# Joining two half inverses in three slots of a hand-ordered attention and MLP kernel

## The chip, the cores and the metric

One NeuronCore of a Trainium2 chip. The metric is device time in microseconds (us) of one execution, lower is better. Three runs of the kernel before stand at 674.85, 675.14 and 677.65; the median is 675.14.

## The reference

A delta rule with memory runs over 768 tokens for 4 x 8 heads of 48 dimensions, and its output is the input of a gated MLP (384 to 1536 to 384):

```python
for t in range(S):
    y[:, :, t] = np.einsum('bhd,bhde->bhe', q[:, :, t], state)
    v_old = np.einsum('bhde,bhd->bhe', state, kt)
    state = state + bt[:, :, :, None] * np.einsum('bhd,bhe->bhde', kt, vt - v_old)
...
gate = 1.0 / (1.0 + np.exp(-(x @ w_gate)))
return (gate * (x @ w_val) @ w_out)
```

with `kt` a row of k divided by its norm. Everything is float32.

## The kernel before

**Work.** The tokens are cut into N = 12 groups of 64 tokens a batch (256 rows of the MLP each). In a group the delta rule becomes matrix work: a Gram matrix of the keys (`gram`, L253), norms (`norms`, L206), the inverse of a triangular matrix of 64 x 64 per head, held as two 32 x 32 blocks on the diagonal (`mt`) and one block beside it (`L`), the corrected values U (`rest` L376 to L394, `updates` L396), the output Y (`rows`, L421), the new state (`advance`, L450) and a transposition of Y into the two-part operand `xx` of the MLP (`flip`, L469). The MLP of a group runs in NF = 12 tiles of 128 hidden units: `gate_val` (18 matmuls, L492), `gated` (sigmoid on ScalarE L497, product on VectorE L498), `split_hi` (L503), `split_lo` (L508) and `outp` (6 matmuls, L518).

**Slots.** The order of every engine's instructions is written out by hand: `slot(s)` (L673) is called for s = 0, 1, 2 ... and each engine works through its own instructions strictly in that order. An even slot issues `gate_val` of tile s/2, then the list `plan[s]`, then `split_lo` of the tile before and `gated` of its own tile, then the list `late[s]`. An odd slot issues `outp` of the tile that is two back, `plan[s]`, `split_hi`, `late[s]`. Slots 0 to 23 run the MLP of group 0, 24 to 47 that of group 1, and so on. In this document "tile 6" is the tile of slot 12, and "tile 12" the first tile of group 1, in slot 24.

**What is in `plan` up to slot 24.** The MLP's weights come as raw words and are converted in the first 21 slots: `converting` (L196) gives 97 steps, some 4.6 a slot, of which two in three run on VectorE (`join` L184, `weight_lo` L194) and one on ScalarE (`weight_hi` L189); `scaled` (L164) gives two more ScalarE passes a piece up to slot 15, a small POOL copy (L176) and the load of a later piece on SP's queue. `gate_val(f)` needs the pieces that were converted one or two slots earlier.

**Group 1's inverse.** For groups 0 and 1 `solve_halves` (L327) inverts two halves of 16 rows and joins them. Norms and halves of group 1 are one generator of NORMS + HALVES = 18 + 40 = 58 steps, which `spread` (L540) deals out evenly over slots 0 to 11. Its last six steps are two copies of the halves into `X` (L353, after a memset of X on POOL, L351), and then the joining:

```python
nc.vector.transpose(mt..., X...)          # L355, and with it
blocks(pz, A, mt)                         # L362: 128 small matmuls, then a step ends
nc.vector.transpose(D..., mt...)          # L365
nc.scalar.copy(Z, pz)                     # L366, a step ends
blocks(pm, D, Z)                          # L362: 128 small matmuls, a step ends
nc.vector.tensor_tensor(out=mt, in0=mt, in1=pm, op=ALU.subtract)   # L370
```

All six fall into slot 10 (the first of them) and slot 11 (the other five), in `plan`, so before `split_lo` and `gated` of slot 10, and before `split_hi` of slot 11. They depend on each other in turn: VectorE, TensorE, ScalarE, TensorE, VectorE.

**What follows for group 1.** `updates(1, 0)`, `(1, 1)` and `(1, 2)` stand in `late` of slots 13, 15 and 17, `rows(1)` and `advance(1)` in slot 19, both `flip(1, c)` in slot 21; `gate_val` of tile 12 in slot 24 needs `xx` of group 1.

**Group 2's inverse** is a single chain of 18 + 66 = 84 VectorE steps (`norms`, `solve` L296) over slots 16 to 32. The share of a slot is weighted by `max(0.1, 1.6 - busy[s])`, and `busy` (a table of extra VectorE work by slot) is filled from `up` and `at_rows`, the slots of U and Y. It ends with the transposition into `mt` (L319), which `updates(2, 0)` in slot 34 needs (L413).

Of the kernel before, what the change touches and what calls it, by code (L numbers as in the profile page):

```python
# [55 lines left out]
def deltanet_gated_mlp(ctx: ExitStack, tc: tile.TileContext, kd, qd, kv, beta, words, out):  # L56
# [107 lines left out]
    def scaled(n):  # L164

        half, lo, hi = words_of(n)
        nc.scalar.activation(lo.bitcast(I32), half, AF.Copy, bias=-4095.5 / 8192, scale=1 / 8192)
        h = hi.bitcast(F32)  # L170
        nc.scalar.activation(h, h, AF.Prelu, scale=2.0 ** -112, alpha=-2.0 ** 32)
        later = n + AHEAD
        if later < len(pieces):

            raw[later] = wt.tile([128, PW, 2], U32, name=f"raw_{later}", tag=f"w{later}")
            nc.gpsimd.tensor_copy(out=raw[later][0:1, 0:1, 0], in_=raw[n][0:1, 0:1, 1])  # L176
            load_piece(later)
# [28 lines left out]
    def norms(g):  # L206


        st = state[g]
        st["gp"] = gp = wk.tile([128, 32, 32], F32, name=f"gp_{g}", tag="gp", bufs=1)  # L210
        nc.vector.transpose(gp.rearrange("q t (c r) -> q t c r", r=2), st["G"].unsqueeze(3).to_broadcast([128, 32, CP, 2]))
        yield
        ss = gp.rearrange("q t c -> q (t c)")[:, 0:32 * 32:33]
        t1, y, t, s, m = (wk.tile([128, 32], F32, name=f"{x}_{g}", tag=x, bufs=1) for x in ("n1", "ny", "nt", "ns", "m"))
        nc.vector.tensor_scalar(out=t1.bitcast(I32), in0=ss.bitcast(I32), scalar1=1, scalar2=None, op0=ALU.logical_shift_right)
        yield
        nc.vector.tensor_scalar(out=y.bitcast(I32), in0=t1.bitcast(I32), scalar1=-1.0, scalar2=float(0x5f375a00), op0=ALU.mult, op1=ALU.add)
        yield
        for _ in range(2):
            nc.vector.scalar_tensor_tensor(out=t, in0=y, scalar=-0.5, in1=y, op0=ALU.mult, op1=ALU.mult)  # L220
            yield
            nc.vector.tensor_tensor(out=t, in0=t, in1=ss, op=ALU.mult)
            yield
            nc.vector.scalar_tensor_tensor(out=y, in0=t, scalar=1.5, in1=y, op0=ALU.add, op1=ALU.mult)
            yield
        nc.vector.tensor_tensor(out=s, in0=y, in1=ss, op=ALU.mult)
        yield
        nc.vector.scalar_tensor_tensor(out=t, in0=s, scalar=-1.0, in1=s, op0=ALU.mult, op1=ALU.mult)
        yield
        nc.vector.tensor_tensor(out=t, in0=t, in1=ss, op=ALU.add)  # L230
        yield
        nc.vector.scalar_tensor_tensor(out=t, in0=t, scalar=0.5, in1=y, op0=ALU.mult, op1=ALU.mult)
        yield
        nc.vector.scalar_tensor_tensor(out=m, in0=t, scalar=EPS, in1=s, op0=ALU.add, op1=ALU.add)
        yield
        nc.vector.tensor_tensor(out=t, in0=m, in1=m, op=ALU.mult)
        yield
        st["gam"] = gam = wk.tile([128, 32], F32, name=f"gam_{g}", tag="gam", bufs=2)
        nc.vector.reciprocal(gam, t)
        yield  # L240
        nc.vector.tensor_tensor(out=gam, in0=gam, in1=st["beta"], op=ALU.mult)
        yield
        st["mq"] = mq = wk.tile([128, CP, 2], F32, name=f"mq_{g}", tag="mq", bufs=1)
        nc.vector.transpose(mq.rearrange("p c r -> p (c r)"), m)
        yield
# [81 lines left out]
    def solve_halves(g):  # L327


        st = state[g]  # L330
        gp, gam = st["gp"], st["gam"]
        X = wk.tile([128, 16, 32], F32, name=f"X_{g}", tag="X", bufs=1)
        H = wk.tile([128, 2, 8, 16], F32, name=f"H_{g}", tag="H", bufs=1)
        gs = wk.tile([128, 2, 16, 16], F32, name=f"gs_{g}", tag="gs", bufs=1)
        A, D, Z = (scratch[:, i] for i in range(3))
        for b in range(2):
            nc.vector.tensor_tensor(out=H[:, b], in0=dmask[:, 8 * b:8 * b + 8, 16 * b:16 * b + 16],
                                    in1=gam[:, 16 * b:16 * b + 16].unsqueeze(1).to_broadcast([128, 8, 16]), op=ALU.mult)
            yield
            nc.vector.scalar_tensor_tensor(out=gs[:, b], in0=gp[:, 16 * b:16 * b + 16, 16 * b:16 * b + 16], scalar=-1.0,  # L340
                                           in1=gam[:, 16 * b:16 * b + 16].unsqueeze(1).to_broadcast([128, 16, 16]), op0=ALU.mult, op1=ALU.mult)
            yield
        for j in range(15, 0, -1):
            k, n = j // 2, 8 - j // 2
            tmp = wk.tile([128, 2, n, j], F32, name=f"tmp_{g}_{j}", tag="tmp", bufs=2)
            nc.vector.tensor_tensor(out=tmp, in0=H[:, :, k:8, j:j + 1].to_broadcast([128, 2, n, j]),
                                    in1=gs[:, :, j:j + 1, 0:j].to_broadcast([128, 2, n, j]), op=ALU.mult)
            yield
            nc.vector.tensor_tensor(out=H[:, :, k:8, 0:j], in0=H[:, :, k:8, 0:j], in1=tmp, op=ALU.add)
            yield  # L350
        nc.gpsimd.memset(X, 0.0)  # L351
        for b in range(2):
            nc.vector.tensor_copy(out=X[:, 8 * b:8 * b + 8, 16 * b:16 * b + 16], in_=H[:, b])  # L353
            yield
        nc.vector.transpose(mt.rearrange("q c (k r) -> q k c r", r=2), X.rearrange("q k (c r) -> q k c r", r=2))  # L355
        pool, tag = (ps_aux, "aux") if g else (ps_gv, "gv")
        pz, pm = (pool.tile([128, CP, 32], F32, name=f"{n}_{g}", tag=tag) for n in ("pz", "pm"))

        def blocks(out, lhsT, rhs):
            for c in range(CP):  # L360
                for r in range(0, 128, 32):
                    nc.tensor.matmul(out=out[r:r + 32, c], lhsT=lhsT[r:r + 32, c], rhs=rhs[r:r + 32, c], start=True, stop=True)  # L362
        blocks(pz, A, mt)
        yield
        nc.vector.transpose(D.rearrange("q c t -> q (c t)"), mt.rearrange("q c t -> q (c t)"))  # L365
        nc.scalar.copy(Z, pz)  # L366
        yield
        blocks(pm, D, Z)
        yield
        nc.vector.tensor_tensor(out=mt, in0=mt, in1=pm, op=ALU.subtract)  # L370
        yield
# [159 lines left out]
    plan = collections.defaultdict(list)  # L531
    late = collections.defaultdict(list)

    def steps(gen, n=1):
        def fn():
            for _ in range(n):
                next(gen, None)
        return fn

    def spread(gen, total, lo, hi, room=lambda s: 1.0):  # L540

        done, upto, whole = 0, 0.0, sum(room(s) for s in range(lo, hi))
        for s in range(lo, hi):
            upto += total * room(s) / whole
            n = total if s == hi - 1 else round(upto)
            plan[s].append(steps(gen, n - done))
            done = n

    def chain(*gens):
        for q in gens:  # L550
            yield from q
# [10 lines left out]
    NORMS, SOLVE, HALVES = 18, 66, 40  # L562
# [52 lines left out]
    spread(conv, 3 * len(pieces) - 11, 0, W - 3)  # L615
    for n in range(11, len(pieces)):
        plan[max(0, (n - 12) * 2 // 3)].append(lambda n=n: scaled(n))
    spread(chain(norms(1), solve_halves(1)), NORMS + HALVES, 0, 12)
    for s in (4, 5):
        plan[s].append(steps(scalings[1], 8))  # L620
    for part in (1, 0):
# [21 lines left out]
    for g in range(N):  # L643
        w = W * (g - 1)
        if g == 0:
            late[3].append(lambda: advance(0))
            continue
        up, at_rows = (13, 19) if g == 1 else (10, 16)
        late[w + 6].append(lambda g=g: rest(g))
        for step in range(3):  # L650
            late[w + up + 2 * step].append(lambda g=g, step=step: updates(g, step))
        late[w + at_rows].append(lambda g=g: rows(g))
        late[w + at_rows].append(lambda g=g: advance(g))
        for c in range(2):
            late[w + at_rows + 2].append(lambda g=g, c=c: flip(g, c))
            busy[w + at_rows + 2] += 0.6
        busy[w + 6] += 1.1
        busy[w + up + 2] += 1.1
        busy[w + at_rows] += 1.1
        busy[w + at_rows + 1] += 1.1  # L660
        if g == 1:
            mask_later(1, 1)
        else:
            if g > 2:
                plan[w - 27].append(lambda g=g: load_group(g))
            gram_later(g, w - 18)
            mask_later(g, w + 1 if g == 2 else w - 12)
            solves.append((g, w - 8 if g == 2 else w - 14, w + 9))
            scaling(g, w - 3 if g == 2 else w - 7)
# [72 lines left out]
```

## Time and profile before

| | |
|---|---|
| median of three runs | 675.14 us |
| time of the profiled execution | 674.84 us |
| its span, first to last instruction | 673.1 us |
| around the span (difference) | 1.74 us |
| TensorE (PE) busy | 617.6 us (92%) |
| VectorE (DVE) busy | 481.3 us (72%) |
| ScalarE (ACT) busy | 322.9 us (48%) |
| GpSimd (POOL) busy | 16.0 us (2%) |
| granted TensorE clock, mean | 0.980 |

The chain of work that ended last runs 77% of the span on PE, 11% on DVE, 5% in issue. A share over the span says little here, as the first 160 us and the rest are two different stages: in the first the weights are converted and the first groups' inverses are made, in the second the MLP runs from weights that lie ready. The profile gives for each instruction when it started, how long it took, how long its engine sat idle before it and what ended that idle time.

### The profile page before, as it was taken

To read this page: it belongs to the slowest core of one execution; us is meant where nothing else is said; L and a number is where in the kernel's file an instruction comes from. 1 tells how busy PE (TensorE), PEld (TensorE's weight loads), DVE (VectorE), ACT (ScalarE), POOL (GpSimd) and SP (SyncE) were. 2 spreads that over 40 slices of the span, in tenths; PEclk is the share of its full clock that TensorE was granted. 3 is DMA by queue.
4 is the path that set the end of the run, shared out by engine and by line. 5 is a ranking of instruction groups with operands and counts; after the bars stand their busy time and mean duration, and the time that the engine had idled before them with its cause. 6 is when DMAs were issued, how large, how long until landed. Compare 5 with 4: busy or idle time off the path is not lost.

```text
span 673.1 us, 24164 instructions
## 1 busy us (share of the span) xinstructions
PE 617.6 (92%) x10504; PEld 595.4 (88%) x10504; DVE 481.3 (72%) x1480; ACT 322.9 (48%) x881; POOL 16.0 (2%) x57
## 2 busy tenths in 40 slices
PE   5278829898999999999999999999999999999996
PEld 4267728788999999999999999999999999999996
DVE  4469857998797797797797787786886886862221
ACT  5748957435535524534534444444444354433322
POOL 5001100000000000000000000000000000000000
PEclk9999869898999999999999999999999999999999
DMA  8565540210210210210220220220220110010101
GB/s 257 182 224 166 196 160 2 81 27 24 82 24 26 83 24 26 81 42 10 81 48 3 81 50 2 81 49 4 81 49 27 58 25 3 1 25 3 24 1 24
DMA packets 17770, 41.07 MB, mean 61 GB/s; under 512 B 4224, under 2 KB 7296, under 8 KB 17664
## 3 DMA queue, kind: packets, MB, share of 16 engines
q1 hardware_dynamic: 17664, 39.53, 20.2%
q8 instruction: 82, 1.34, 0.8%
q14 instruction: 24, 0.20, 0.1%
HBM read 34.80 MB, written 4.72 MB: 59 GB/s over the span
## 4 chain that ended last, share of the span: by engine, by line
PE 77%; DVE 11%; issue 5%; ACT 3%; DMA 2%; SPq 1%; POOL 0%; ACTq 0%; DVEq 0%; POOLq 0%
PE gv L492 41%; PE po L518 22%; PE pu L413 3%; DVE w L194 2%; PE yy L439 2%; PE yy L442 2%; PE pp L286 1%; PE pk L382 1%; DVE u L184 1%; DMA raw<-in_words_dram 1%; PE pd L460 1%; PE pk L405 1%; PE pt L478 1%; PE pg L262 1%; DVE tmp L314 1%
## 5 line engine op out<-in xcount | busy, mean ns | idle before, releaser
L492 PE MATMUL gv<-xx,w 128*128 128x256 f32 x2592 | 343.7, 287 | 7.0 <-DVE w L194 5.0
L492 PEld LDWEIGHTS gv<-xx,w 128*128 128x128 f32 x2592 | 335.2, 194 | 10.4 <-DVE w L194 5.8
L518 PE MATMUL po<-w,h 128*128 128x384 f32 x864 | 182.7, 346 | 0.7 <-DVE h L508 0.7
L497 ACT ACTIVATE sg<-gv 128x256 f32<-128x256 f32 x144 | 55.3, 384 | 198.5 <-PE gv L492 198.3
L518 PEld LDWEIGHTS po<-w,h 128*128 128x128 f32 x864 | 145.5, 189 | 5.3 <-DVE h L508 1.8
L498 DVE TENSOR_TENSOR sg<-sg,gv 128x256 f32<-128x256 f32 x144 | 60.2, 418 | 76.3 <-ACT sg L497 75.9
L503 ACT CAST h<-sg 128x256 fp32r<-128x256 f32 x144 | 58.4, 405 | 69.0 <-DVE sg L498 67.5
L317 DVE TENSOR_TENSOR X<-X,tmp 128x126 f32<-128x126 f32 (+22 forms) x310 | 79.1, 255 | 9.8
L314 DVE TENSOR_TENSOR tmp<-X,gp 128x126 f32<-128x126 f32 (+22 forms) x310 | 78.8, 254 | 9.0
L508 DVE TENSOR_TENSOR h<-sg,h 128x256 fp32r<-128x256 f32 x144 | 60.0, 416 | 27.5 <-ACT h L503 27.5
L419 ACT COPY su<-pu 32x384 f32<-32x384 f32 x92 | 43.3, 471 | 13.6 <-PE pu L413 12.3
L250 ACT ACTIVATE kv<-kv,mq 128x48 f32<-128x48 f32 x192 | 48.1, 330 | 0.0
L467 DVE TENSOR_TENSOR su<-su,pd 48x384 f32<-48x384 f32 x40 | 22.1, 552 | 21.1 <-PE pd L460 20.6
L270 ACT COPY G<-pg 32x256 f32<-32x256 f32 (+1 forms) x72 | 26.5, 368 | 18.5 <-PE pg L262 17.2
L291 DVE TENSOR_TENSOR kqp<-pp,pmask 64x512 f32<-64x512 f32 x48 | 32.1, 686 | 1.2 <-PE pp L286 0.2
L393 DVE TENSOR_TENSOR R<-kv,pk 128x384 f32<-128x384 f32 x44 | 22.4, 550 | 1.8 <-PE pk L382 1.8
L189 ACT CAST w<-u 128x384 fp32r<-128x384 f32 x36 | 17.7, 512 | 11.2 <-DVE u L184 11.1
L413 PE MATMUL pu<-R,mt 32*32 32x48 f32 x1408 | 19.7, 202 | 3.0 <-DVE mt L319 1.9
L413 PEld LDWEIGHTS pu<-R,mt 32*32 32x32 f32 x1408 | 16.6, 105 | 6.4 <-issue 2.3
L362 PE MATMUL pz<-mt,scratch 32*32 32x32 f32 x256 | 3.9, 236 | 19.3 <-DVE mt L355 19.3
L362 PEld LDWEIGHTS pz<-mt,scratch 32*32 32x32 f32 x256 | 3.7, 151 | 19.8 <-issue 19.8
L262 PE MATMUL pg<-kqp 48*64 48x64 f32 x768 | 16.2, 235 | 5.2 <-DMA kqp<-in_kd_dram 5.2
(86 smaller groups left out, 476.4 us busy)
## 6 DMA issues: line engine op xcount, KB each, us to landing
raw<-in_words_dram SPq DMA_DIRECT2D x36, 384.0 KB, 4.1
kv<-in_kv_dram SPq DMA_DIRECT2D x24, 384.0 KB, 5.2
kqp<-in_qd_dram SPq DMA_DIRECT2D x24, 256.0 KB, 3.8
kqp<-in_kd_dram SPq DMA_DIRECT2D x24, 192.0 KB, 3.6
out_dram<-ot SPq DMA_DIRECT2D x48, 96.0 KB, 2.2
beta<-in_beta_dram SPq DMA_DIRECT2D x12, 16.0 KB, 4.5
```

The lines of the kernel that those rows point to most:

```text
L250: nc.scalar.activation(V[:, c], V[:, c], AF.Copy, scale=mq[:, c, 0:1])
L291: nc.vector.tensor_tensor(out=kq[t:t + 64, sec], in0=pp[e][t:t + 64], in1=pmask[t:t + 64, e].unsqueeze(1).to_broadcast([64, J, C]), op=ALU ...
L314: nc.vector.tensor_tensor(out=tmp, in0=X[:, k:16, j:j + 1].to_broadcast([128, n, j]), in1=gp[:, j:j + 1, 0:j].to_broadcast([128, n, j]), o ...
L317: nc.vector.tensor_tensor(out=X[:, k:16, 0:j], in0=X[:, k:16, 0:j], in1=tmp, op=ALU.add)
L413: nc.tensor.matmul(out=pu[0 if g else x][r:r + 32, j], lhsT=mt[r:r + 32, e * J + j], rhs=R[e][r:r + 32, j], start=True, stop=True)
L419: nc.scalar.copy(su[r:r + 32, 3 if x else e], pu[0][r:r + 32])
L492: nc.tensor.matmul(out=pg[:, o], lhsT=parts[w, f][:, a, k * 128:(k + 1) * 128], rhs=x[b][:, k], start=(k == 0 and q == 0), stop=(k == KC - ...
L497: nc.scalar.activation(h, st["gv", f][:, 0], AF.Sigmoid)
L498: nc.vector.tensor_tensor(out=h, in0=h, in1=st["gv", f][:, 1], op=ALU.mult)
L503: nc.scalar.copy(hh[:, 0], st["sg", f])
L508: nc.vector.tensor_tensor(out=hh[:, 1], in0=st["sg", f], in1=hh[:, 0].bitcast(F32), op=ALU.subtract)
L518: nc.tensor.matmul(out=po[s], lhsT=hh[:, a, ts], rhs=parts["o", f][:, w], start=(f == 0 and q == 0), stop=(f == NF - 1 and q == 2))
```

## The change

The first 55 of the 58 steps are dealt out over slots 0 to 10 (five a slot), so that slot 10 ends with the transposition L355 and the first 128 matmuls. Step 56 (L365 and L366) goes to the end of slot 11 (`late`), step 57 (the second 128 matmuls) to the end of slot 12 (`late`), step 58 (L370) into `plan` of slot 13. U, Y and the flips of group 1 move by one slot: 14, 16, 18 for the updates, 20 for `rows` and `advance`, 22 for the flips. Through `busy` this also changes how the 84 steps of group 2's inverse are dealt out.

```diff
-    spread(chain(norms(1), solve_halves(1)), NORMS + HALVES, 0, 12)
+    first = chain(norms(1), solve_halves(1))
+    spread(first, NORMS + HALVES - 3, 0, 11)
+    for s in (11, 12):
+        late[s].append(steps(first))
+    plan[13].append(steps(first))
...
-        up, at_rows = (13, 19) if g == 1 else (10, 16)
+        up, at_rows = (14, 20) if g == 1 else (10, 16)
```

## Rows read from the trace of the kernel before

**Rows 1.** The page, busy tenths in 40 slices of 16.8 us.

```profile
PE   5278829898999999999999999999999999999996
...
DVE  4469857998797797797797787786886886862221
```

**Rows 2.** Waits of PE, 50 to 170 us: us in total, times, longest.

```profile
PE pz L362 <- DVE mt L355: 10.1, 1, 10.1
```

**Rows 3.** Waits of PE, 166 us to the end.

```profile
PE pd L460 <- issue: 0.7, 2, 0.4
```

**Rows 4.** Waits of DVE, 84 to 160 us.

```profile
DVE mt L370 <- PE pm L362: 6.2, 1, 6.2
DVE sg L498 <- ACT sg L497: 5.0, 3, 2.7
DVE X L353 <- POOL X L351: 1.3, 1, 1.3
```

**Rows 5.** Timeline, slots 10 to 12: start, length, instruction, idle before and releaser.

```profile
90.91 0.23 DVE L353 COPY X<-H 128x128 f32<-128x128 f32 x1 [1.30 <-POOL X L351]
...
93.50 0.71 DVE L355 STREAM_TRANSPOSE mt<-X 128x512 f32<-128x512 f32 x1
94.25 0.71 DVE L365 STREAM_TRANSPOSE scratch<-mt 128x512 f32<-128x512 f32 x1
...
94.36 1.93 PE L362 MATMUL pz<-mt,scratch 32*32 32x32 f32 x128 [10.14 <-DVE mt L355]
...
99.75 1.38 PE L362 MATMUL pm<-scratch 32*32 32x32 f32 x83 [1.91 <-issue]
...
101.06 3.29 PE L492 MATMUL gv<-xx,w 128*128 128x256 f32 x18
101.17 0.69 DVE L370 TENSOR_TENSOR mt<-mt,pm 128x512 f32<-128x512 f32 x1 [6.21 <-PE pm L362]
```

**Rows 6.** Timeline of DVE and ACT, slots 12 to 22.

```profile
104.99 0.42 DVE L498 TENSOR_TENSOR sg<-sg,gv 128x256 f32<-128x256 f32 x1 [1.26 <-ACT sg L497]
...
106.57 1.96 ACT L419 COPY su<-pu 32x384 f32<-32x384 f32 x4
...
111.68 0.42 DVE L498 TENSOR_TENSOR sg<-sg,gv 128x256 f32<-128x256 f32 x1 [2.75 <-ACT sg L497]
```

**Rows 7.** Timeline of DVE, slots 21 to 34.

```profile
134.78 1.02 DVE L481 TENSOR_TENSOR xx<-pt,xx 128x384 fp32r<-128x384 f32 x2 [0.49 <-ACT xx L480]
...
137.79 0.41 DVE L498 TENSOR_TENSOR sg<-sg,gv 128x256 f32<-128x256 f32 x1
...
158.99 0.71 DVE L319 STREAM_TRANSPOSE mt<-X 128x512 f32<-128x512 f32 x1
```

**Rows 8.** Timeline of PE, slots 24 to 36.

```profile
135.85 2.31 PE L492 MATMUL gv<-xx,w 128*128 128x256 f32 x17 [0.29 <-DVE xx L481]
...
154.56 1.22 PE L518 MATMUL po<-w,h 128*128 128x384 f32 x6
155.62 2.32 PE L492 MATMUL gv<-xx,w 128*128 128x256 f32 x18
159.85 0.88 PE L413 MATMUL pu<-R,mt 32*32 32x48 f32 x64 [1.91 <-DVE mt L319]
160.66 1.96 PE L518 MATMUL po<-w,h 128*128 128x384 f32 x6
162.41 3.23 PE L492 MATMUL gv<-xx,w 128*128 128x256 f32 x18
```

**Rows 9.** Stretches: length, busy us of PE, PEld, DVE, ACT, POOL, PEclk, DMA share, GB/s.

```profile
134.00:138.00 4.00, 2.68 (x20) 2.34 (x19) 3.27 (x13) 3.19 (x12) 0.00 (x0) 1.00 0.00 0
...
162.40:165.60 3.20, 3.20 (x23) 3.07 (x22) 1.71 (x8) 1.15 (x3) 0.00 (x0) 0.67 0.02 5
```

**Rows 10.** The page: engines' busy time and instructions; the instruction queue (packets, MB, share).

```profile
PE 617.6 (92%) x10504; PEld 595.4 (88%) x10504; DVE 481.3 (72%) x1480; ACT 322.9 (48%) x881; POOL 16.0 (2%) x57
...
q8 instruction: 82, 1.34, 0.8%
```

## The prediction

> **What bounds the kernel now.** I read first the busy tenths [rows 1]. PE stands at 9 from the eleventh slice on, that is from about 168 us; in the slices before, DVE is the fuller engine and PE has holes. The waits of PE confirm the border: after 166 us it waited 0.7 us in all [rows 3], before that it waited 10.1 us at one place, the first small matmuls of the joining [rows 2]. So whatever PE gains before about 166 us, it keeps to the end; nothing behind that can give or take much.
>
> Next I asked what holds PE before the border. The 10.1 us are not a price by themselves: PE had run ahead of DVE, which converts the weights, and only stood until DVE came. What counts is the time that DVE stands still, because DVE's list up to the transposition of group 2's inverse (158.99 us) ends last: PE's matmuls on it wait for it until 159.85 us, with 1.91 us idle [rows 7, 8]. The waits of DVE between 84 and 160 us are 12.5 us in three kinds [rows 4], and 0.5 for the flips [rows 7]. The largest, 6.2 us, is the change's subject: at 94.96 us DVE has made both transpositions, then PE does 128 small matmuls, ACT copies, PE does 128 more, and only at 101.17 us can DVE subtract [rows 5]. In the second 128 PE itself stands 1.91 us with nothing that the profile names as releaser. Behind it come 1.26 and 2.75 us, DVE waiting for the sigmoids of tiles 6 and 7 [rows 6], and the flips' 0.49. From the joining on that makes 6.21 + 1.26 + 2.75 + 0.49 = 10.7 us of idle DVE.
>
> The profiled execution took 674.84 us (673.1 of span and 1.74 around it), 0.3 us under the median of the three runs; I make the sum against 674.84. A measurement of this kernel tells about 0.5%, 3.4 us, from no change.
>
> **The change, part by part.** No instruction is added or taken away, and none of the moved steps issues a DMA. The loads of group 3 in slot 21, on SP's queue, wait for `rows(1)` and `advance(1)` as before, and their data is used some ten slots later: 0. POOL's memset keeps its place behind slot 10's small copies, and DVE still waits for it; two small steps move ahead of slot 10, and I allow 0.4 us for them (0 to 0.5).
>
> *First transposition and first 128 matmuls, now in slot 10.* At 90.91 us DVE starts the first copy into X. Between that and L365 at 94.25 us it does the second copy, L355, the pair L508 and L498 and three conversion steps [rows 5]. The same seven now stand in another order: L355 follows the two copies and starts at about 91.4. PE's 128 matmuls run from 92.2 to 94.15, 2.1 us earlier. L365 still starts at 94.25.
>
> *Slots 11 and 12.* In place of waiting, DVE goes on with slot 12's three conversion steps and the split, 1.9 us, to 96.9. It needs tile 6's sigmoid next. PE, in order, has `outp` of tile 3 and then tile 6 behind the 128 matmuls, and has been idle, so I price both as the rows after an idle stretch show them: 1.75 us (160.66 to 162.41) and 3.2 us [rows 5, 8]. That ends at 99.1, the sigmoid 0.4 later. DVE waits 2.6 us here, where before it waited 6.21 and 1.26.
>
> *Second 128 matmuls (end of slot 12) and subtraction (slot 13).* They need D and Z, ready at about 95, so PE runs them right behind tile 6: 99.1 to 101.3. DVE, after the product of 0.34 and three conversion steps, comes to the subtraction at about 101.4. Wait: 0, if the 1.91 us of [rows 5] do not recur. Queued behind a late subtraction would be all of slot 14's conversion, for which `gate_val` waits. Why the stall goes: instructions come by a queue of their own, 82 packets of 16 KB for PE's 21,008 matmuls and weight loads, or 256 instructions a packet [rows 10]; the joining hands PE 512 of them in under 4 us, and now `outp` and tile 6 stand between the halves. The other end is that the stall stays with the second half: 1.9 us. I take 0, as nothing else in the rows would hold PE there. The Trainium skill's page "Runtime: NRT & Kernel Launch", section "Instruction fetch mechanics", says that blocks of 256 instructions are streamed ahead and that crossing one is mostly hidden. By that page the 1.91 us would be of another kind and would stay; the trace has a hole of just that size, so I do not go by it in the sum, and the case has its place among the rivals.
>
> *Tile 7's sigmoid.* Before, DVE waited 2.75 us because ACT had the four copies of `updates(1, 0)`, 1.96 us, ahead of it [rows 6]. They now stand in `late` of slot 14, behind that sigmoid. What is left is 0.8; DVE comes earlier against ACT's two `scaled` passes, so I take 1.2 (0.8 to 2.75).
>
> *Updates, rows and flips one slot later.* The matmuls and copies are the same. PE has slack there, since it waits for conversions. The price falls on the flips: L481 now stands behind slot 22's pair and steps. Before, DVE finished L481 at 135.80 and slot 22 at 138.20, 2.4 us [rows 7]. By the new `busy`, 30 of the 84 steps are done by then and not 33, three steps or 0.7 us less; by the end of slot 30 the counts are equal (70). So `xx` is ready 1.7 us later in DVE's list. The flips' wait of 0.5 us I leave in.
>
> *Sum for DVE.* 10.7 - 2.6 - 0 - 1.2 - 0.5 - 0.4 = 6.0 us earlier.
>
> *Sum for PE.* Tile 12 starts at 135.85 + 1.7 - 6.0 = 131.55. Its wait, 1.3 us now (2.68 us busy of 4.00), grows to about 3, and an idle stretch of 1.91 us at 158 was followed by a granted clock of 0.67 (part of the stretch at 1.2 GHz, part at 2.4), while tile 12's present wait was not [rows 8, 9]. The low level costs 0.7 on `outp` (1.75 against 1.06 start to start) and 0.9 on the tile (3.23 against 2.32), 1.6 us [rows 8]. From tile 12 to the end of slot 34 PE has 22.1 us of work without a hole (135.85 to 157.94). So it reaches `updates(2, 0)` at 131.55 + 22.1 + 1.6 = 155.25. DVE's transposition ends at 159.70 - 6.0 = 153.7: no wait is left there, and the 1.6 us that the low level cost behind it are gone. The gain is 159.85 - 155.25 + 1.6 = 6.2 us, and the time 674.84 - 6.2 = 668.6.
>
> **The rivals.**
> (1) *The clock stays up at tile 12.* For it: the hole there may be shorter than 3 us or fall as the present one did [rows 9]. Then PE reaches slot 34 at 153.65, DVE at 153.7, and the gain is 6.1 + 1.6 = 7.7: 667.1.
> (2) *The stall of 1.9 us stays with the second 128 matmuls.* DVE waits 1.8 at the subtraction, its sum falls to 4.2, the gain to 4.4: 670.4. For it: its cause is not shown. Against: the hole lies in the middle of two like blocks that ran back to back.
> (3) *The wait is exchanged for others.* ACT's wait for tile 7 stays at 2.75 as well, and tiles 8 and 9 each add 0.5 (what the flips cost DVE now) because PE is behind: 1.55 + 1.0 more, the gain 1.9: 672.9, no change that can be told. For it: both pz and tile 6 now lie in one queue on PE that DVE waits for. Against: in slots 16 to 20 DVE had no wait for PE or ACT [rows 4, 6, 7].
> (4) *PE takes over at the low clock and the kernel gets slower.* Each new hole (before pz, tile 10, tile 12) could start a stretch at 1.2 GHz, and with PE's work per two slots raised by 1.6 us it, not DVE, would set the pace from slot 11 on. Eleven tiles to slot 34 make 17.6 us, of which 3.2 are in the sum: 6.2 - 14.4 = -8.2, or 683.0. It decides from about six tiles beyond the two counted. Against: after the hole of 158 us the level was back for the second tile [rows 8, 9].
>
> **How the numbers follow.** My forecast has 0.60, (1) 0.13, (2) 0.13, (3) 0.10, (4) 0.04. Forecast, (1) and (2) are faster by over 0.5% of 675.14, which is below 671.8: 0.86. (3) is the same: 0.10. Slower: 0.04. The range runs from 666.7, (1) with POOL's 0.4 not needed, to 671.6, (2) with 1.2 us of the doubt on tile 7's sigmoid; it leaves out (3), (4) and little else.
>
> **What would show it.** Right: DVE's 6.2 us wait for the second matmuls gone or under 0.5; a wait of 2 to 3 us for tile 6's sigmoid; the second 128 matmuls without a hole; tile 12's wait for L481 near 3 us with the clock below 1 behind it; PE's wait for group 2's `mt` gone and `updates(2, 0)` near 155. Wrong: DVE's idle sum behind 90 us above 8, or `updates(2, 0)` after 158, or a new wait of PE behind 166 us.

## The result and the profile after

The changed kernel takes 668.62 us (median of 4 runs, 668.24 to 669.96) against 675.0 of the kernel before (674.78 to 677.65): a ratio of 0.9905 with a 95% interval of 0.9884 to 0.9927. The forecast was 668.6, faster. The profiled execution took 668.93 us; its span is 667.2 us, 5.9 less than before.

The waits of DVE in the changed kernel, 84 to 155 us, answer to [rows 4]:

```profile
DVE sg L498 <- ACT sg L497: 4.4, 3, 2.7
DVE X L353 <- POOL X L351: 1.6, 1, 1.6
DVE kqp L291 <- PE pp L286: 1.1, 1, 1.1
DVE w L194 <- ACT w L189: 0.5, 1, 0.5
```

(Each line: us in total, times, longest.) The 6.2 us before the subtraction (L370) are gone. Two small waits are new: 1.1 us for the masks of group 2 in slot 25 (L291) and 0.5 us in slot 16 (L194). The timeline of slots 10 to 14 shows the joining in its new places ([rows 5, 6]; start, length, instruction, idle before and releaser):

```profile
91.50 0.36 DVE L353 COPY X<-H 128x128 f32<-128x128 f32 x2 [1.63 <-POOL X L351]
91.90 0.71 DVE L355 STREAM_TRANSPOSE mt<-X 128x512 f32<-128x512 f32 x1
...
94.69 0.71 DVE L365 STREAM_TRANSPOSE scratch<-mt 128x512 f32<-128x512 f32 x1
...
99.94 0.42 DVE L498 TENSOR_TENSOR sg<-sg,gv 128x256 f32<-128x256 f32 x1 [2.71 <-ACT sg L497]
...
102.41 0.68 DVE L370 TENSOR_TENSOR mt<-mt,pm 128x512 f32<-128x512 f32 x1
...
105.20 0.42 DVE L498 TENSOR_TENSOR sg<-sg,gv 128x256 f32<-128x256 f32 x1 [0.71 <-ACT sg L497]
```

DVE stands 2.71 us for tile 6, comes to the subtraction without a wait, and stands 0.71 us for tile 7 where it stood 2.75. TensorE in the same slots and up to slot 34 ([rows 5, 8]):

```profile
92.76 1.93 PE L362 MATMUL pz<-mt,scratch 32*32 32x32 f32 x128 [8.89 <-DVE mt L355]
94.62 2.29 PE L518 MATMUL po<-w,h 128*128 128x384 f32 x6
96.70 2.73 PE L492 MATMUL gv<-xx,w 128*128 128x256 f32 x18
99.36 1.29 PE L362 MATMUL pm<-scratch 32*32 32x32 f32 x128
...
128.54 0.39 PE L492 MATMUL gv<-xx,w 128*128 128x256 f32 x1 [1.51 <-ACT xx L480]
131.09 3.44 PE L492 MATMUL gv<-xx,w 128*128 128x256 f32 x17 [2.17 <-DVE xx L481]
134.34 1.61 PE L518 MATMUL po<-w,h 128*128 128x384 f32 x6
...
152.16 2.32 PE L492 MATMUL gv<-xx,w 128*128 128x256 f32 x18
154.61 0.88 PE L413 MATMUL pu<-R,mt 32*32 32x48 f32 x64
```

The second block (pm) runs without a hole. Tile 12 waits 3.7 us in two parts and then runs slowly. The granted clock of these stretches (columns as in [rows 9]) is low behind both idle times and comes back, here for the joining and then for tile 12:

```profile
94.60:96.70 2.10, 2.10 (x13) 2.09 (x7) 2.07 (x5) 1.82 (x4) 0.00 (x0) 0.50 0.96 294
96.70:99.30 2.60, 2.60 (x19) 2.53 (x18) 0.54 (x2) 1.51 (x4) 0.00 (x0) 0.82 0.16 41
99.30:100.60 1.30, 1.30 (x131) 1.20 (x129) 0.66 (x2) 1.07 (x3) 0.00 (x0) 1.00 0.04 13
```

```profile
133.00:134.40 1.40, 1.40 (x9) 1.40 (x8) 1.26 (x5) 0.00 (x0) 0.00 (x0) 0.50 0.00 0
134.40:135.90 1.50, 1.50 (x11) 1.25 (x10) 1.43 (x6) 0.44 (x2) 0.00 (x0) 0.73 0.00 0
135.90:137.00 1.10, 1.10 (x66) 1.03 (x65) 0.11 (x1) 0.35 (x1) 0.00 (x0) 1.00 0.07 15
```

Group 2's first update starts at 154.61, 5.24 us sooner than at 159.85 [rows 8], with no idle time printed before it. PE ends the tile ahead of it at 154.48, and DVE's timeline has its input ready at 154.46, so both lists arrive together:

```profile
153.75 0.71 DVE L319 STREAM_TRANSPOSE mt<-X 128x512 f32<-128x512 f32 x1
```

Behind it PE's only waits are 1.5 us in all (0.7 before, [rows 3]), so all but 0.8 us of the gain stays.

### The profile page after: what moved, and what is told of

Read it like the earlier page. It is cut to its first block, busy times and chain, and to the rows that moved or that the text cites. A ratio compares the mean times of both kernels' runs of the same rounds, so it can differ in the third digit from the quotient of the medians.

```text
span 667.2 us, 24164 instructions
## 1 busy us (share of the span) xinstructions
PE 614.4 (92%) x10504; PEld 593.6 (89%) x10504; DVE 481.5 (72%) x1480; ACT 323.1 (48%) x881; POOL 15.7 (2%) x57
## 4 chain that ended last, share of the span: by engine, by line
PE 81%; issue 11%; DVE 4%; POOL 2%; ACT 1%; ACTq 0%; POOLq 0%
PE gv L492 43%; PE po L518 23%; PE pu L413 2%; PE pp L286 2%; PE yy L439 2%; PE pk L382 2%; PE yy L442 2%; PE pg L262 1%; PE pd L460 1%; PE pk L405 1%; PE pt L478 1%; DVE w L194 1%; POOL raw L176 1%; ACT raw L171 1%; PE pz L362 1%
## 5 line engine op out<-in xcount | busy, mean ns | idle before, releaser
L291 DVE TENSOR_TENSOR kqp<-pp,pmask 64x512 f32<-64x512 f32 x48 | 32.1, 686 | 2.2 <-PE pp L286 1.2
L184 DVE SCALAR_TENSOR_TENSOR u<-raw 128x384 uint32<-128x384 uint32 x36 | 19.9, 556 | 0.9
L262 PEld LDWEIGHTS pg<-kqp 48*64 48x64 f32 x768 | 14.6, 149 | 6.3 <-DMA kqp<-in_kd_dram 4.5
```

The source lines that it names most:

```text
L262: nc.tensor.matmul(out=pg[e][t:t + 64, j], lhsT=kq[r:r + D, x, j], rhs=kq[r:r + D, x, j], start=True, stop=True)
L291: nc.vector.tensor_tensor(out=kq[t:t + 64, sec], in0=pp[e][t:t + 64], in1=pmask[t:t + 64, e].unsqueeze(1).to_broadcast([64, J, C]), op=ALU ...
```

## The experiments

All are compared with the kernel before, which stood at a median of 675.88 for the first four and 674.79 for the others. The two groups were timed apart, so versions are compared with one another by their ratios as well as by their medians. As a second measure I give when group 2's transposition L319 starts in the one profile of each version. The first copy into X, ahead of the joining, starts between 90.12 and 97.30 us in the ten profiles; where it is far off, I give the time from it to L319. Lines that are added move the line numbers of the last versions down by up to five; the tile names stay.

**The joining alone** (U, Y and flips back in slots 13 to 21).

```diff
-        up, at_rows = (14, 20) if g == 1 else (10, 16)
+        up, at_rows = (13, 19) if g == 1 else (10, 16)
```

> The joining in three slots alone; U, Y and the flips of group 1 stay in slots 13 to 21. My theory (VectorE's idle time up to group 2's inverse is the currency, and the two halves of the edit need each other): the wait for the second small matmuls goes and tile 6's sigmoid is waited for 2.7 us, but the four copies of the first update now stand ahead of tile 7's sigmoid behind a later subtraction, so VectorE waits 4 to 5 us there in place of 0.7. Gain over the kernel before 1.5 to 2.5 us, 672.5 to 673.5, and TensorE's wait for group 2's inverse is still there (1 to 2 us). Rival A (the joining alone is the gain, U and Y are only moved out of its way): 668 to 669.5.

671.93 us, ratio 0.9955 (0.9926 to 0.9984): 3.0 us by the ratio and 4.0 by the medians, more than the 1.5 to 2.5 that I expected and well short of rival A. L319 starts at 156.59, 2.4 sooner than before. DVE's timeline at tile 7 shows what holds it:

```profile
109.23 0.42 DVE L498 TENSOR_TENSOR sg<-sg,gv 128x256 f32<-128x256 f32 x1 [4.71 <-ACT sg L497]
```

The update's copies stand ahead of that sigmoid and now wait for a later subtraction: on ScalarE they start at 104.14, after 2.58 us of waiting for the update's matmuls, and the sigmoid at 108.82. In the profiled execution, 3.68 us shorter than the one before, the rest of the gain came by the clock. PE's timeline still has the hole before group 2's update:

```profile
157.45 0.88 PE L413 MATMUL pu<-R,mt 32*32 32x48 f32 x64 [1.84 <-DVE mt L319]
```

but in the stretch behind it (length, busy us of PE, PEld, DVE, ACT, POOL, PEclk, DMA share, GB/s) the granted clock stayed at 1.00, where before it fell to 0.67 [rows 9]:

```profile
157.00:165.00 8.00, 7.55 (x225) 7.25 (x226) 7.25 (x20) 3.87 (x9) 0.00 (x0) 1.00 0.01 2
```

**The later U, Y and flips alone** (the joining as before).

```diff
-    first = chain(norms(1), solve_halves(1))
-    spread(first, NORMS + HALVES - 3, 0, 11)
-    for s in (11, 12):
-        late[s].append(steps(first))
-    plan[13].append(steps(first))
+    spread(chain(norms(1), solve_halves(1)), NORMS + HALVES, 0, 12)
```

> The joining as before in slots 10 and 11, only U, Y and the flips of group 1 one slot later. My theory: the wait of 6.2 us stays, tile 7's wait falls from 2.75 to about 1.2, the flips cost 1.7 us in VectorE's list and the wait before tile 12 grows to 3 us or more with a low clock behind it; group 2's inverse is ready about 1.5 us earlier. Gain 0.5 to 2.5 us: 672.5 to 674.5. Rival A: 675, no change. Rival B (one slot less between flips and tile 12 is a cost of its own): 676 or more.

673.75 us, ratio 0.9976 (0.9955 to 0.9997), inside the expected range; rival B falls, and A lies at the edge of the interval. But the way there was another: L319 was to be 1.5 us sooner and starts at 159.77, 0.8 later than before. Tile 7's wait is 1.29, but tile 6's is 2.06 and the masks cost 1.9. That the time is still no longer goes with PE, which reaches the update with next to no wait, and the stretch behind (160.6 to 165.0) has a granted clock of 1.00.

```profile
160.62 0.88 PE L413 MATMUL pu<-R,mt 32*32 32x48 f32 x64 [0.16 <-DVE mt L319]
...
162.60 2.32 PE L492 MATMUL gv<-xx,w 128*128 128x256 f32 x18
```

Before, that tile took 3.23 [rows 8]. So the time of this version is no measure of DVE's list. The two parts move L319 by -2.4 and +0.8 alone and by -5.24 together. The difference, 3.6 us, is about what tile 7's wait shows: 4.71 with the joining alone, 0.71 with both.

**The flips in slot 21** (the rest as changed).

```diff
-            late[w + at_rows + 2].append(lambda g=g, c=c: flip(g, c))
+            late[w + at_rows + (1 if g == 1 else 2)].append(lambda g=g, c=c: flip(g, c))
```

> As the changed kernel, but both flips of group 1 in slot 21 (U and Y stay in 14 to 20; the table of extra work is unchanged). My theory: xx is ready about 1.2 us earlier, TensorE's wait before tile 12 falls to 2 to 3 us, but VectorE's transposition of group 2's inverse is where it was (about 153.5), so TensorE waits there again for 1 to 2 us: 667.5 to 669.5, about as the changed kernel. Rival (the later flips cost the changed kernel their 1.7 us and the low clock in full): 665.5 to 667.

667.98 us (666.29 to 670.64), ratio 0.9901 (0.987 to 0.9933): by the time not told apart from the changed kernel. The wait for the masks is gone, which I had not foreseen, and DVE's list is shorter: from the first copy into X to L319 it takes 60.56 us (94.04 to 154.60), in the changed kernel 62.25 (91.50 to 153.75). Of these 1.7 us the masks are 1.1; tile 6's wait is 2.19 and no longer 2.71, as that tile ran with the clock back (1.00; it took 2.31 us). The wait of 1 to 2 us that I expected for group 2's inverse did not come. The rival is not excluded: the list gained what it says, and two of the four executions lie in its range.

**The two blocks back to back** (steps 56 and 57 at the end of slot 10).

```diff
-    for s in (11, 12):
-        late[s].append(steps(first))
+    late[10].append(steps(first, 2))
```

> As the changed kernel, but steps 56 and 57 both at the end of slot 10: the second 128 small matmuls follow the first with only the ScalarE copy between them, as before the change; the subtraction stays in slot 13. If the hole of 1.91 us is instruction loading for two blocks that follow each other: a hole of 1.5 to 2.5 us inside the second block again, tile 6's sigmoid waited for 6 to 7 us, 671.5 to 673. Rival (the hole was something else that the two blocks only happened to meet): no hole, tile 6 waited for 4.5 to 5 us, 670 to 671.

671.24 us, ratio 0.995 (0.9932 to 0.9968). The time lies between the two forecasts, but PE's timeline decides: no hole, only the wait for ScalarE's copy.

```profile
93.00 1.93 PE L362 MATMUL pz<-mt,scratch 32*32 32x32 f32 x128 [8.89 <-DVE mt L355]
95.63 2.25 PE L362 MATMUL pm<-scratch 32*32 32x32 f32 x128 [0.69 <-ACT scratch L366]
97.81 2.29 PE L518 MATMUL po<-w,h 128*128 128x384 f32 x6
99.90 3.29 PE L492 MATMUL gv<-xx,w 128*128 128x256 f32 x18
```

So my reason for the hole, two blocks of 256 instructions in a row, does not hold as I put it. Tile 6 is waited for 6.08 us, since the second block, tile 3's output and tile 6 run in a row, the first two at a granted clock of 0.50 and the tile at 0.65. This prices the second block ahead of tile 6: 2.6 us against the changed kernel's 668.62, 3.0 by the ratios.

**Tile 3's output ahead of the first block** (the first 128 matmuls become a step of their own, in slot 11).

```diff
+        if g:
+            yield
         pool, tag = (ps_aux, "aux") if g else (ps_gv, "gv")
...
+    plan[11].append(steps(first))
     for s in (11, 12):
```

> As the changed kernel, but the first 128 small matmuls stand in slot 11 behind the output matmuls of tile 3 and no longer ahead of them. My theory (VectorE's 2.7 us wait for tile 6's sigmoid is TensorE working off, at the low clock, what is queued behind the first small matmuls): the output matmuls run in TensorE's idle time, tile 6 is done 1.7 us sooner, the wait falls to 0.7 to 1.4 us, and the whole comes 1.0 to 1.8 us below the changed kernel's 668.6 (ratio to before about 0.988). Rival (the wait is ScalarE's own list, which passes two pieces ahead of that sigmoid): wait and time as in the changed kernel.

667.67 us (666.23 to 674.13), ratio 0.9911 (0.9885 to 0.9936): not told apart from the changed kernel. The expectation was missed: the wait falls only to 2.10 (in the profile, which is of the slowest execution, 674.13 us). Without the output matmuls in front of it, tile 6 itself ran longer, 4.21 us where it took 2.73 (PE's timeline):

```profile
98.56 1.93 PE L364 MATMUL pz<-mt,scratch 32*32 32x32 f32 x128 [7.25 <-DVE mt L355]
100.42 4.21 PE L494 MATMUL gv<-xx,w 128*128 128x256 f32 x18
```

The rival falls as well, since ScalarE waits 0.73 us for tile 6 before that sigmoid. What is queued there mattered less than PE's slow start: the granted clock was 0.51 over 100.4 to 104.6 us.

**The memset early** (POOL clears X at the head of the halves and not behind slot 10's copies).

```diff
         A, D, Z = (scratch[:, i] for i in range(3))
+        if g:
+            nc.gpsimd.memset(X, 0.0)
...
-        nc.gpsimd.memset(X, 0.0)
+        if g == 0:
+            nc.gpsimd.memset(X, 0.0)
```

> As the changed kernel, but POOL's memset of X for group 1 is issued at the head of the halves (slot 3 or 4) and not behind slot 10's small copies. My theory (idle VectorE time before group 2's inverse comes straight off the end): the wait of 1.6 us for POOL goes, nothing takes its place, 1.3 to 1.6 us below the changed kernel (ratio to before about 0.988). Rival (the time is taken back by the wait for tile 6's sigmoid, since ScalarE and TensorE are no sooner): that wait grows to 3.5 us or more, time as in the changed kernel.

666.61 us, ratio 0.9896 (0.9857 to 0.9934): by the time alone not told apart from the changed kernel (0.9884 to 0.9927). The list shows the gain: L319 starts at 152.03, 1.7 us sooner than in the changed kernel, and the waits of DVE (84 to 160 us) have no line of POOL; the longest for a sigmoid is 2.3, so the rival falls:

```profile
DVE sg L501 <- ACT sg L500: 4.4, 4, 2.3
DVE kqp L291 <- PE pp L286: 1.1, 1, 1.1
DVE w L194 <- ACT w L189: 0.4, 1, 0.4
```

**All three** (output first, memset early, flips in slot 21; the three diffs above together).

> Both of these and the flips in slot 21. My theory: the three add up, since each takes idle time out of VectorE's list at another place: 3.5 to 5 us below the changed kernel, 663.5 to 665 (ratio to before 0.982 to 0.985). Rival (TensorE's own list from tile 12 to slot 34 becomes the bound): 665.5 to 667.

664.65 us (664.11 to 665.87), ratio 0.9855 (0.9838 to 0.9872): 4.0 us below the changed kernel's 668.62, as expected (3.4 by the ratios, just short of the 3.5). The intervals of this version and the changed kernel do not meet, and this is the best version tried. L319 starts at 150.60, and in PE's timeline the update comes right behind, still waiting for DVE, so the rival falls:

```profile
151.46 0.88 PE L418 MATMUL pu<-R,mt 32*32 32x48 f32 x64 [0.22 <-DVE mt L319]
```

**More work for VectorE in slot 28.**

```diff
...
+    for _ in range(4):
+        plan[28].append(lambda: nc.vector.tensor_tensor(out=dum[1], in0=dum[0], in1=dum[0], op=ALU.add))
```

> The changed kernel with four more VectorE additions of 128 x 384 (0.55 us each, 2.1 us together, their result is not used) in slot 28, between tile 12 and group 2's inverse. It measures whether VectorE's list still sets when TensorE gets group 2's inverse. My theory (both lists reach slot 34 together: 154.46 and 154.48 in the profile): 1.8 to 2.1 us more, and up to 1.6 on top if the low clock follows TensorE's new wait: 670.4 to 672.3. Rival (TensorE alone sets the pace from tile 12 on): no change, 668.3 to 669.

(The two tiles `dum` are set up ahead of slot 0, with one memset on POOL.) 671.44 us, ratio 0.9951 (0.9926 to 0.9977), 2.8 above the changed kernel by the medians and 3.1 by the ratios. From the first copy into X to L319 it takes 64.66 us (92.57 to 157.23) where the changed kernel took 62.25: 2.4 us more for the four additions, and PE's timeline shows a wait nearly as long:

```profile
158.09 0.88 PE L413 MATMUL pu<-R,mt 32*32 32x48 f32 x64 [2.30 <-DVE mt L319]
```

So DVE's list still reaches slot 34 no sooner than PE's, and time added to it there goes to the end. The rival falls.

## Why the prediction was right, and where its steps were not

*DVE's idle time is the currency.* Right, and shown from both sides: taking 1.6 us of it away (memset) brought L319 1.7 us forward, though by its time alone that version is not told apart, and adding 2.4 us of work put 2.8 us on the time. The later U, Y and flips alone show the limit: there the list came 0.8 us later and the time was no longer.

*First block in slot 10.* Forecast 91.4 for L355, 92.2 for the matmuls, 94.25 for L365; they came at 91.90, 92.76 and 94.69. The 0.4 us that I allowed for POOL are 0.3 of longer wait and a later start.

*Tile 6, 2.6 us.* Measured 2.71. The parts differ: tile 3's output cost more (2.08 us start to start, allowed 1.75) and tile 6 less (2.73, allowed 3.2), since the clock came back within it (0.82). With the output out of the way 2.10 of the 2.71 us stayed, so most of the term is PE's slow start.

*Subtraction, 0.* Right, but for a reason that did not hold: the two blocks back to back had no hole either. (Nor does PE get their 512 instructions in under 4 us: the rows of before give the two blocks 1.93 + 0.85 + 1.38 = 4.2 us of work.) What made the 1.91 us is open (below).

*Tile 7, 1.2 us.* Measured 0.71, under my lower bound of 0.8. The mechanism, the update's four copies, is shown by the 4.71 us with the joining alone.

*Flips.* I left 0.5 us in, and it is 0. Missing from the sum were the masks' 1.1 us (PE, late at tile 12, brings slot 25's matmuls late) and 0.5 us in slot 16. So DVE came 5.24 us forward (158.99 to 153.75) and not 6.0.

*PE from tile 12.* Forecast 131.55, a wait of about 3 and 1.6 us of low clock; measured 131.09, 3.7 and 1.5 (3.44 against 2.31 on the tile, 1.61 against 1.22 on the output). The update was forecast at 155.25 and came at 154.61; as forecast, no wait was left there.

*The low clock that is saved behind slot 34, 1.6 us.* This is the weak term. Before, the stretch behind the hole of 1.91 us ran low; but behind 1.84 us in the joining alone and 2.30 us with the added work it did not. The two profiles compared have it, and the span's 5.9 us are 5.24 + 1.6 - 0.8 of longer waits for issue later on - 0.1. Over other executions it is a chance, not a certain saving. What makes the clock fall behind one such idle time and not behind another is not shown.

*The total.* That the median came within 0.1 us of the forecast is luck. In the profile the gain up to the update was 5.24 us where I had 4.6 (159.85 - 155.25), the clock gave the 1.6, and 0.8 of longer waits for issue behind 166 us had been put at nothing; these errors nearly cancel.

*Rivals.* (1) did not come: the clock fell at tile 12. (2) did not come: the hole did not stay with the second block. It stood beside the Trainium skill's page "Runtime: NRT & Kernel Launch", section "Instruction fetch mechanics", which says that crossing a block of instructions is mostly hidden; no run here shows whether the 1.91 us were such a crossing. (3) did not come; it has its nearest likeness in the joining alone. (4) did not come: PE was at 1.00 again by 136 us.

## What to carry to other kernels

When a chain hops between engines inside lists that are worked off in order, put a slot of other work between its links, and move the consumers by as much: here one half of the edit gained 2.4 us on the list that bounds, the other half lost 0.8, and both together gained 5.2. Price such an edit by the idle time of the engine whose list ends last, not by the longest wait in the profile: TensorE's wait for the first block went from 10.1 us only to 8.9 and the kernel still won 1%. Then look for the next idle time on the same list (here a memset behind an unrelated queue), and expect several small ones to add up.

## What the runs showed of the hardware that was not expected

The hole in the second block has a fixed place in PE's list and a changing length. In group 0's joining, at 29 us (34 in one), it stood behind 93 of 128 matmuls in all ten profiles, 1.1 to 2.2 us long. Here PE's timeline of the kernel before, and then of the flips in slot 21:

```profile
29.01 1.49 PE L362 MATMUL pm<-scratch 32*32 32x32 f32 x93 [0.69 <-ACT scratch L366]
31.87 0.74 PE L362 MATMUL pm<-scratch 32*32 32x32 f32 x35 [1.36 <-issue]
```

```profile
29.10 1.49 PE L362 MATMUL pm<-scratch 32*32 32x32 f32 x93 [0.69 <-ACT scratch L366]
32.82 0.74 PE L362 MATMUL pm<-scratch 32*32 32x32 f32 x35 [2.23 <-issue]
```

In one (tile 3's output first) the block before has such a hole too, 4.6 us long behind 94 matmuls; that execution reached the first copy into X at 97.30, the others at 94.04 or sooner, and took 674.13 us where the median of its kernel is 667.67:

```profile
26.74 1.50 PE L364 MATMUL pz<-mt,scratch 32*32 32x32 f32 x94 [9.73 <-DVE mt L355]
32.79 0.74 PE L364 MATMUL pz<-mt,scratch 32*32 32x32 f32 x34 [4.55 <-issue]
34.20 1.49 PE L364 MATMUL pm<-scratch 32*32 32x32 f32 x93 [0.68 <-ACT scratch L368]
36.89 0.74 PE L364 MATMUL pm<-scratch 32*32 32x32 f32 x35 [1.20 <-issue]
```

The two places lie 34 + 93 = 127 matmuls apart, 254 instructions with their weight loads, close to the 256 of one packet that the prediction works out from [rows 10]. For group 1 the hole stood behind 45 matmuls in the two kernels with the old joining, 1.91 and 1.15 us. A fixed place and a length that changes from execution to execution fit instruction loading, but that was not tried by itself and is not shown; why the back-to-back version has no such hole stays open.

For group 1 the small matmuls go with the clock: the second block took 2.25 us at a granted clock of 0.50 (back to back) and 1.29 at 1.00 (changed kernel). Group 0's do not fit this: its second block has 1.49 + 0.74 us of work where the profile prints a clock of 1.00 (29.0 to 30.5 us in the kernel before). That stays open too.
